# Attention with one query over 4096 keys: values matmuls on four column groups, a K pool of two buffers and a V pool of one

## The chip, the cores and the metric

One core of one Trainium2 chip. The metric is the device time in microseconds (us) of one execution, as the median of a kernel's runs. Single executions of one kernel mostly lie within 0.3% of each other. A profiled run's span is 1.7 us shorter than its reported time.

## The reference

```
B, H, Sq, Skv, Dh = 8, 32, 1, 4096, 128            # q, k, v in bfloat16
scores = einsum('bhqd,bhkd->bhqk', q, k) * Dh ** -0.5
out    = einsum('bhqk,bhkd->bhqd', softmax(scores), v)
```

There are 256 heads with one query each. K and V are 268.4 MB each and every byte is used once, so the kernel is a stream of 536.9 MB with some arithmetic beside it.

## The kernel before

Eight heads make a tile. A tile of K or V is 128 partitions x 256 rows x 128 numbers, 8.39 MB or 64 KiB per partition; there are 32 tiles of each (numbered 0 to 31). The kernel has three such buffers (192 KiB per partition) in SBUF, and its pool hands them out in turn to K and V. DVE multiplies K by the query and halves the sum over d, PE finishes that sum with identity matmuls, DVE and ACT make the softmax weights, and PE multiplies the weights by V ("values"): 64 matmuls per tile with 32 output columns each, then "pick" matmuls gather the right quarter of the 32 x 512 result.

```
SLOTS = 3
LAST = (8, 4)
...
    kv_pool = ctx.enter_context(tc.tile_pool(name="kv_pool", bufs=SLOTS))
...
    cuts = { ...                                    # pieces of a load, in rows of 256
        ("k", NT - 1): [C // 4, C // 4, C // 2],
        ("v", NT - 2): [C // 4] * 4,
        ("v", NT - 1): [C // 4] + [C // 8] * 4 + [24, 16, 12, *LAST],
    }
    def load(kind, t):
        src = k_t if kind == "k" else v_t
        buf = kv_pool.tile([P, C, D], BF16, name=f"{kind}t", tag="kv")
        ...                                         # one DMA per piece, all from SyncE
...
    def values_of(t, lo, hi):
        ...
        for c0 in range(lo, hi, CB):                # CB = 4 rows, 8 heads: 32 columns
            nc.tensor.matmul(
                avs[t][:], lhsT=w[:, c0 : c0 + CB, :], rhs=vt[:, c0 : c0 + CB, :],
                start=(c0 == 0), stop=...,
            )
...
        for t in range(NT):                         # Q = C // 4
            load("k", t + 1); load("v", t)
            product(t, 0, Q);      values_of(t - 2, 3 * Q, ...);  sum_over_d(t, 0)
            values_of(t - 2, ..., C); copy_of(t - 2)
            product(t, Q, 2 * Q);  sum_over_d(t, 1);  scores_of(t, 0)
            result_of(t - 2);      values_of(t - 1, 0, Q)
            product(t, 2 * Q, 3 * Q); sum_over_d(t, 2);  scores_of(t, 1)
            values_of(t - 1, Q, 2 * Q)
            product(t, 3 * Q, C);  sum_over_d(t, 3);  scores_of(t, 2); scores_of(t, 3)
            weights_of(t);         values_of(t - 1, 2 * Q, 3 * Q)
```

The loop is shortened here: the guards for the first and last tiles are left out. The order in it is the order on each engine. Values of one tile are spread over the time of two.

## Time and profile before

| | before |
|---|---|
| time, median of 6 runs | 1254.86 us (1254.75 to 1255.53) |
| span of the profiled run | 1253.2 us |
| first load packet / last V byte landed | 1.8 / 1249.2 us |
| one 64 KB packet on one DMA engine | 2.42 us (median of 7296) |

The first fence holds lines of the page of the kernel before: busy time by engine with its share of the span; the bandwidth in 40 equal slices of the span; the load queue with its share of the 16 DMA engines' time; two groups of instructions (busy us, mean ns of one, then the idle time before them and what ended it); the chain.

```profile
span 1253.2 us, 8139 instructions
PE 844.0 (67%) x3307; PEld 326.9 (26%) x3307; DVE 967.2 (77%) x531; ACT 341.1 (27%) x641; POOL 3.1 (0%) x17
...
GB/s 404 435 434 434 435 434 435 431 434 434 435 432 436 434 434 433 427 431 433 434 429 435 434 435 431 436 434 431 434 423 435 434 425 436 436 426 427 424 429 326
...
q1 hardware_dynamic: 12224, 536.94, 99.3%
...
DMA 59%; PE 32%; DVE 8%; ACT 1%; issue 0%; another core or an unknown queue 0%; SPq 0%
...
L173 DVE TENSOR_TENSOR kt<-kt,qb 128x8192 bf16<-128x8192 bf16 x128 | 565.1, 4415 | 137.2 <-DMA kt<-in_k_dram 130.3
L249 PE MATMUL av<-vt,w 128*32 128x512 bf16 x2045 | 529.8, 419 | 99.5 <-DMA vt<-in_v_dram 97.8
...
vt<-in_v_dram SPq DMA_DIRECT2D x30, 26.1
kt<-in_k_dram SPq DMA_DIRECT2D x27, 26.1
```

The load queue holds the 16 DMA engines for 99.3% of the span, and the bandwidth line is flat from the second slice to the last but one. DVE and PE both wait for loads, and yet the queue never runs empty. The chain gives PE 32%, but that is a matter of how it is followed back: a load waits for a buffer, the buffer for PE, PE for the load before it. What decides is whether the queue ever runs empty, and here it does not. The last two lines say that a whole load lands 26.1 us after its issue; as a tile takes 19.4 us to move, it was issued some 7 us before the queue would have emptied. I call that time the **lead** of a load.

The second fence is busy time by stretch at the end of the kernel before (window in us from the span's start, then the length, busy time and number of instructions per engine, granted PE clock, DMA share, GB/s).

```profile
core 0: us, PE busy (x) PEld busy (x) DVE busy (x) ACT busy (x) POOL busy (x), PEclk, DMA share, GB/s
1190.00:1228.00 38.00, 34.06 (x145) 13.85 (x144) 30.33 (x17) 10.43 (x18) 0.00 (x0) 0.90 1.01 428
1228.00:1233.00 5.00, 5.00 (x24) 2.15 (x23) 1.79 (x5) 2.59 (x9) 0.00 (x0) 1.00 0.98 413
1233.00:1249.00 16.00, 14.37 (x74) 6.39 (x72) 0.16 (x1) 7.25 (x25) 0.26 (x1) 1.00 0.84 345
1249.00:1254.00 5.00, 1.30 (x17) 0.90 (x15) 0.00 (x0) 0.94 (x2) 0.00 (x0) 0.85 0.00 1
```

DMA is full up to the last stretch, and PE works at full clock beside the last V tile. The fence is the timeline of PE in the middle of the kernel before (start, length, then the idle time before it).

```profile
606.59 5.30 PE L249 MATMUL av<-vt,w 128*32 128x512 bf16 x16 [3.51 <-DMA vt<-in_v_dram]
611.82 1.90 PE L188 MATMUL ps<-kt,ident 128*128 128x512 bf16 x8
613.65 3.63 PE L249 MATMUL av<-vt,w 128*32 128x512 bf16 x16
617.21 1.90 PE L188 MATMUL ps<-kt,ident 128*128 128x512 bf16 x8
619.04 5.35 PE L249 MATMUL av<-vt,w 128*32 128x512 bf16 x24
```

Sixteen values matmuls take 3.63 us once PE's clock is up and 5.30 us after idle time: 0.22 to 0.33 us each.

### The profile page before, as it was taken

Reading aid. Unit: us, or ns where it says so; the run is one execution under the profiler, and the core shown is the slowest. Engines: PE = TensorE matmul, PEld = TensorE weight load, DVE = VectorE, ACT = ScalarE, POOL = GpSimd, SP = SyncE. Lnnn points to the kernel's source line nnn. Section 1 sums busy time; section 2 is a strip of 40 time slices with the busy share of each in tenths; the row PEclk is TensorE's granted clock in tenths of the full one; section 3 lists DMA queues with packets and bytes.
Section 4 is the critical chain, followed back from the end, with each engine's and each line's share of the span. In section 5 each row is a group of like instructions: output and inputs, shape, how many; then the busy total and the mean of one; then the engine's idle time right before and its main releaser. Section 6 shows DMA issues by size and latency. Waiting matters only on the chain.

```text
span 1253.2 us, 8139 instructions
## 1 busy us (share of the span) xinstructions
PE 844.0 (67%) x3307; PEld 326.9 (26%) x3307; DVE 967.2 (77%) x531; ACT 341.1 (27%) x641; POOL 3.1 (0%) x17
## 2 busy tenths in 40 slices
PE   2466765768667685666765667765677667775788
PEld 0122222223222232222322222222222222222333
DVE  7877887777977779777788777886778877878991
ACT  0323033331233321333213322033220333313333
POOL 0000000000000000000000000000000000000000
PEclk8689787788778887788977888788887887887889
DMA  9999999999999999999999999999999999999997
GB/s 404 435 434 434 435 434 435 431 434 434 435 432 436 434 434 433 427 431 433 434 429 435 434 435 431 436 434 431 434 423 435 434 425 436 436 426 427 424 429 326
DMA packets 12598, 537.53 MB, mean 429 GB/s; under 512 B 1936, under 2 KB 2064, under 8 KB 2576
## 3 DMA queue, kind: packets, MB, share of 16 engines
q1 hardware_dynamic: 12224, 536.94, 99.3%
q8 instruction: 26, 0.43, 0.1%
q10 hardware_dynamic: 336, 0.07, 0.0%
q14 instruction: 12, 0.10, 0.0%
HBM read 536.94 MB, written 0.07 MB: 428 GB/s over the span
## 4 chain that ended last, share of the span: by engine, by line
DMA 59%; PE 32%; DVE 8%; ACT 1%; issue 0%; another core or an unknown queue 0%; SPq 0%
DMA vt<-in_v_dram 58%; PE av L249 22%; PE ps L188 10%; DVE kt L173 5%; DVE kt L176 2%; DMA q_all<-in_q_dram 1%; DVE sc L200 1%; ACT w L233 0%; DVE pmax L210 0%; DVE spread L212 0%; DVE nmax L217 0%; PE op L295 0%; ACT comb L284 0%; DVE bias L221 0%
## 5 line engine op out<-in xcount | busy, mean ns | idle before, releaser
L173 DVE TENSOR_TENSOR kt<-kt,qb 128x8192 bf16<-128x8192 bf16 x128 | 565.1, 4415 | 137.2 <-DMA kt<-in_k_dram 130.3
L249 PE MATMUL av<-vt,w 128*32 128x512 bf16 x2045 | 529.8, 419 | 99.5 <-DMA vt<-in_v_dram 97.8
L188 PE MATMUL ps<-kt,ident 128*128 128x512 bf16 x1024 | 303.6, 450 | 273.6 <-DVE kt L176 273.3
L233 ACT ACTIVATE w<-sc,bias 128x256 bf16<-128x256 f32 (+1 forms) x264 | 301.1, 1557 | 532.3 <-DVE bias L221 532.3
L249 PEld LDWEIGHTS <-w 128*32 128x32 bf16 x2045 | 206.6, 105 | 418.5 <-issue 238.9
L176 DVE TENSOR_TENSOR kt<-kt 128x4096 bf16<-128x4096 bf16 x128 | 293.3, 2292 | 4.4
L188 PEld LDWEIGHTS <-ident 128*128 128x128 bf16 x1024 | 105.5, 109 | 469.1 <-issue 347.8
L200 DVE TENSOR_REDUCE sc<-ps 128x64 f32<-128x512 f32 x128 | 87.6, 685 | 114.9 <-PE ps L188 114.9
L233 ACT ACTIVATION_READ_ACCUMULATOR w<-sc,bias 128x1 f32 x264 | 130.8, 495 | 0.0
L284 ACT ACTIVATE comb<-av 32x512 bf16<-32x512 f32 x32 | 19.1, 597 | 236.6 <-PE qh L157 158.6
L306 ACT ACTIVATE stage<-op,rz 16x128 bf16<-16x128 f32 x16 | 5.7, 358 | 112.1 <-DVE rz L271 111.3
L163 PE MATMUL qp<-qg,heads 8*128 8x128 bf16 x32 | 6.9, 214 | 24.8 <-ACT qg L161 24.8
L210 DVE TENSOR_REDUCE pmax<-sc 128x1 f32<-128x256 f32 x32 | 13.4, 420 | 1.1
L161 ACT ACTIVATE qg<-qh 8x128 bf16<-8x128 f32 x32 | 8.1, 252 | 18.3 <-PE qh L157 18.3
L157 PE MATMUL qh<-q_all,ident 128*8 128x128 bf16 x32 | 7.2, 224 | 8.4 <-DMA q_all<-in_q_dram 8.4
L295 PE MATMUL op<-comb,pick 32*16 32x128 bf16 x128 | 12.3, 215 | 0.2 <-ACT comb L284 0.2
L271 DVE RECIPROCAL rz<-zp 16x1 f32<-16x1 f32 x16 | 2.3, 147 | 12.1 <-PE zp L263 12.1
L165 ACT ACTIVATE qb<-qp 128x128 bf16<-128x128 f32 x32 | 8.9, 278 | 9.6 <-PE qp L163 9.6
L212 DVE TENSOR_SCALAR spread<-same,pmax 128x32 f32<-128x32 f32 x32 | 7.7, 242 | 1.1
L295 PEld LDWEIGHTS <-pick 32*16 32x16 bf16 x128 | 6.6, 83 | 7.0 <-issue 6.6
L221 DVE TENSOR_SCALAR bias<-own,nmax 128x8 f32<-128x8 f32 x32 | 7.4, 230 | 1.1
L217 DVE TRANSPOSE_TENSOR_REDUCE nmax<-spread 128x1 f32<-128x32 f32 x32 | 6.8, 212 | 1.1
(29 smaller groups left out, 18.1 us busy)
## 6 DMA issues: line engine op xcount, KB each, us to landing
kt<-in_k_dram SPq DMA_DIRECT2D x8, 4096.0 KB, 25.5
vt<-in_v_dram SPq DMA_DIRECT2D x5, 2048.0 KB, 27.1
kt<-in_k_dram SPq DMA_DIRECT2D x4, 2048.0 KB, 15.2
vt<-in_v_dram SPq DMA_DIRECT2D x4, 1024.0 KB, 25.8
vt<-in_v_dram SPq DMA_DIRECT2D x1, 768.0 KB
vt<-in_v_dram SPq DMA_DIRECT2D x1, 512.0 KB, 21.8
vt<-in_v_dram SPq DMA_DIRECT2D x30, 26.1
kt<-in_k_dram SPq DMA_DIRECT2D x27, 26.1
```

Of the source, the lines that this page charges most:

```text
L161: nc.scalar.activation(out=qg[:], in_=qh[:], func=ACT.Copy)
L165: nc.scalar.activation(out=qb[:, 0, :], in_=qp[:], func=ACT.Copy)
L173: nc.vector.tensor_tensor(out=part, in0=part, in1=qb[:].to_broadcast([P, MC, D]), op=ALU.mult)
L176: nc.vector.tensor_tensor(out=part[:, :, 0 : D // 2], in0=part[:, :, 0 : D // 2], in1=part[:, :, D // 2 : D], op=ALU.add,)
L188: nc.tensor.matmul(ps[:], lhsT=ident[:], rhs=kt[:, u * UC : (u + 1) * UC, s * DS : (s + 1) * DS], start=(s == 0), stop=(s == n - 1),)
L200: nc.vector.tensor_reduce(out=scs[t][:, u * UC : (u + 1) * UC], in_=sums.pop((t, u))[:], axis=AX.X, op=ALU.add)
L210: nc.vector.tensor_reduce(out=pmax[:], in_=sc[:], axis=AX.X, op=ALU.max)
L212: nc.vector.tensor_scalar(out=spread[:], in0=same[:], scalar1=pmax[:, 0:1], scalar2=-scale, op0=ALU.add, op1=ALU.mult,)
L233: nc.scalar.activation(out=w[:, c0 : c0 + n, g], in_=sc[:, c0 : c0 + n], func=ACT.Exp, bias=bias[:, g : g + 1], scale=scale, accum_out=esu ...
L249: nc.tensor.matmul(avs[t][:], lhsT=w[:, c0 : c0 + CB, :], rhs=vt[:, c0 : c0 + CB, :], start=(c0 == 0), stop=(c0 + CB == (C if t < NT - 1 e ...
L284: nc.scalar.activation(out=comb[:], in_=avs.pop(t)[:], func=ACT.Copy)
L295: nc.tensor.matmul(ops[n][:], lhsT=pick[:, m, r, :], rhs=comb[:, m * D : (m + 1) * D], start=(r == 0 and m == 0), stop=(r == R - 1 and m = ...
```

## The change

The intent: fill the array. A values matmul has 32 output columns, so four of them fit side by side on four column groups, each into its own quarter of the PSUM tile's partitions. With the values of a tile done in one short burst, V needs its buffer for hardly longer than the load itself, so one V buffer is enough and K can have two.

```
-SLOTS = 3
+KB, VB = 2, 1
+TG = 4
-LAST = (8, 4)
+LAST = 4
...
-    kv_pool = ctx.enter_context(tc.tile_pool(name="kv_pool", bufs=SLOTS))
+    k_pool = ctx.enter_context(tc.tile_pool(name="k_pool", bufs=KB))
+    v_pool = ctx.enter_context(tc.tile_pool(name="v_pool", bufs=VB))
...
-        ("v", NT - 2): [C // 4] * 4,
-        ("v", NT - 1): [C // 4] + [C // 8] * 4 + [24, 16, 12, *LAST],
+        ("v", NT - 1): [C // 2, C // 4, C // 8, C // 16, C // 32, LAST, LAST],
...
         for c0 in range(lo, hi, CB):
+            j = c0 // CB % TG
             nc.tensor.matmul(
-                avs[t][:], lhsT=w[:, c0 : c0 + CB, :], rhs=vt[:, c0 : c0 + CB, :],
-                start=(c0 == 0), stop=(c0 + CB == (C if t < NT - 1 else C - NL)),
+                avs[t][j * AG : (j + 1) * AG, :], lhsT=w[:, c0 : c0 + CB, :],
+                rhs=vt[:, c0 : c0 + CB, :], start=(c0 < CB * TG), stop=(c0 + CB * TG >= end),
             )
...
     def copy_of(t):                                # last tile: half by ACT, half by DVE
-        nc.scalar.activation(out=comb[:], in_=avs.pop(t)[:], func=ACT.Copy)
+        n = CB if t < NT - 1 else CB // 2
+        nc.scalar.activation(out=comb[:, 0:n, :], in_=av[:, 0:n, :], func=ACT.Copy)
+        if n < CB:
+            nc.vector.tensor_copy(out=comb[:, n:CB, :], in_=av[:, n:CB, :])
...
+            v_last = t >= NT - 2
...
             sum_over_d(t, 1)
             scores_of(t, 0)
+            if t > 0 and not v_last:
+                values_of(t - 1, 0, C)             # the whole burst, behind the 2nd score sum
+                copy_of(t - 1)
...
             sum_over_d(t, 3)
             scores_of(t, 2)
+            if t > 0 and v_last:
+                values_of(t - 1, 0, C)             # last two tiles: behind the 4th
             scores_of(t, 3)
```

All values of tiles t-2 and t-1 that stood between these lines go. The copied tile is 128 x 512 instead of 32 x 512, at the same number of pick matmuls. A second accumulator for the last softmax sums, and some pieces of the last rows, go too.

More of the change, by code (lines that the diff above doesn't have):

```diff
@@ L48 @@
     TB = 32
-    NL = sum(LAST)
-    assert NH % P == 0 and P % G == 0 and TB % PH == 0 and C % CB == 0
+    AG = CB * G
+    assert TG * AG == P and NH % P == 0 and P % G == 0 and TB % PH == 0 and C % CB == 0
     q_n = q.rearrange("b h o d -> (b h o) d").rearrange("(x p) d -> p x d", p=P)
@@ L104 @@
     )
-    pick = consts.tile([CB * G, CB, R, RG], BF16, name="pick")
+    pick = consts.tile([P, CB, R, RG], BF16, name="pick")
     nc.gpsimd.memset(pick[:], 0.0)
-    nc.gpsimd.affine_select(
-        out=pick[:], in_=pick[:], pattern=[[-G, CB], [G, R], [-1, RG]],
-        compare_op=ALU.not_equal, fill=1.0, base=0, channel_multiplier=1,
-    )
-    nc.gpsimd.affine_select(
-        out=pick[:], in_=pick[:], pattern=[[-G, CB], [0, R], [0, RG]],
-        compare_op=ALU.is_ge, fill=0.0, base=0, channel_multiplier=1,
-    )
-    nc.gpsimd.affine_select(
-        out=pick[:], in_=pick[:], pattern=[[G, CB], [0, R], [0, RG]],
-        compare_op=ALU.is_ge, fill=0.0, base=G - 1, channel_multiplier=-1,
-    )
+    for j in range(TG):
+        part = pick[j * AG : (j + 1) * AG, :, :, :]
+        nc.gpsimd.affine_select(
+            out=part, in_=part, pattern=[[-G, CB], [G, R], [-1, RG]],
+            compare_op=ALU.not_equal, fill=1.0, base=0, channel_multiplier=1,
+        )
+        nc.gpsimd.affine_select(
+            out=part, in_=part, pattern=[[-G, CB], [0, R], [0, RG]],
+            compare_op=ALU.is_ge, fill=0.0, base=0, channel_multiplier=1,
+        )
+        nc.gpsimd.affine_select(
+            out=part, in_=part, pattern=[[G, CB], [0, R], [0, RG]],
+            compare_op=ALU.is_ge, fill=0.0, base=G - 1, channel_multiplier=-1,
+        )
     ones = consts.tile([P, 1], F32, name="ones")
     nc.vector.memset(ones[:], 1.0)
-    late = consts.tile([P, R, G], F32, name="late")
-    nc.vector.memset(late[:], 0.0)
-    w_last = consts.tile([P, NL, RG], BF16, name="w_last")
+    w_last = consts.tile([P, LAST, RG], BF16, name="w_last")
     nc.gpsimd.memset(w_last[:], 0.0)
@@ L141, in load @@
         src = k_t if kind == "k" else v_t
-        buf = kv_pool.tile([P, C, D], BF16, name=f"{kind}t", tag="kv")
+        pool = k_pool if kind == "k" else v_pool
+        buf = pool.tile([P, C, D], BF16, name=f"{kind}t", tag=kind)
         c0 = 0
@@ L227, in weights_of @@
         esum = esums[t // R]
-        n = C // 2 if t == NT - 1 else C
-        for c0 in range(0, C, n):
-            if c0 > 0:
-                esum = late
-            for g in range(G):
-                nc.scalar.activation(
-                    out=w[:, c0 : c0 + n, g], in_=sc[:, c0 : c0 + n], func=ACT.Exp,
-                    bias=bias[:, g : g + 1], scale=scale, accum_out=esum[:, t % R, g : g + 1],
-                )
+        for g in range(G):
+            nc.scalar.activation(
+                out=w[:, :, g], in_=sc[:], func=ACT.Exp, bias=bias[:, g : g + 1], scale=scale,
+                accum_out=esum[:, t % R, g : g + 1],
+            )
         ws[t] = w
         if t == NT - 1:
-            nc.gpsimd.tensor_copy(out=w_last[:, :, RG - G : RG], in_=w[:, C - NL : C, :])
+            nc.gpsimd.tensor_copy(out=w_last[:, :, RG - G : RG], in_=w[:, C - LAST : C, :])
     avs = {}
@@ L246, in values_of @@
         if lo == 0:
-            avs[t] = ps_v.tile([CB * G, CB * D], F32, name="av", tag="av")
+            avs[t] = ps_v.tile([P, CB * D], F32, name="av", tag="av")
+        end = C if t < NT - 1 else C - LAST
         for c0 in range(lo, hi, CB):
+            j = c0 // CB % TG
             nc.tensor.matmul(
-                avs[t][:], lhsT=w[:, c0 : c0 + CB, :], rhs=vt[:, c0 : c0 + CB, :],
-                start=(c0 == 0), stop=(c0 + CB == (C if t < NT - 1 else C - NL)),
+                avs[t][j * AG : (j + 1) * AG, :], lhsT=w[:, c0 : c0 + CB, :],
+                rhs=vt[:, c0 : c0 + CB, :], start=(c0 < CB * TG), stop=(c0 + CB * TG >= end),
             )
@@ L260, in norm_of @@
         zp = ps_z.tile([RG, 1], F32, name="zp", tag="zp")
-        parts = [esums.pop(n)] + ([late] if n == NQ - 1 else [])
-        for i, e in enumerate(parts):
-            nc.tensor.matmul(
-                zp[:], lhsT=e.rearrange("p r g -> p (r g)"), rhs=ones[:],
-                start=(i == 0), stop=(i == len(parts) - 1),
-            )
+        nc.tensor.matmul(
+            zp[:], lhsT=esums.pop(n).rearrange("p r g -> p (r g)"), rhs=ones[:],
+            start=True, stop=True,
+        )
         zps[n] = zp
@@ L273 @@
     combs = {}
-    def last_rows(n, lo, hi):
-        for i in range(lo, hi):
-            nc.tensor.matmul(
-                ops[n][:], lhsT=w_last[:, i, :], rhs=loads["v", NT - 1][:, C - NL + i, :],
-                start=False, stop=(i == NL - 1),
-            )
-    def copy_of(t):
-        comb = small.tile([CB * G, CB * D], BF16, name="comb", tag="comb")
-        nc.scalar.activation(out=comb[:], in_=avs.pop(t)[:], func=ACT.Copy)
+    def copy_of(t):
+        comb = small.tile([P, CB, D], BF16, name="comb", tag="comb")
+        av = avs.pop(t)[:].rearrange("p (m d) -> p m d", d=D)
+        n = CB if t < NT - 1 else CB // 2
+        nc.scalar.activation(out=comb[:, 0:n, :], in_=av[:, 0:n, :], func=ACT.Copy)
+        if n < CB:
+            nc.vector.tensor_copy(out=comb[:, n:CB, :], in_=av[:, n:CB, :])
         combs[t] = comb
@@ L292, in result_of @@
         if t == NT - 1:
-            last_rows(n, 0, LAST[0])
+            for i in range(LAST):
+                nc.tensor.matmul(
+                    ops[n][:], lhsT=w_last[:, i, :], rhs=loads["v", t][:, C - LAST + i, :],
+                    start=False, stop=False,
+                )
         for m in range(CB):
             nc.tensor.matmul(
-                ops[n][:], lhsT=pick[:, m, r, :], rhs=comb[:, m * D : (m + 1) * D],
-                start=(r == 0 and m == 0), stop=(r == R - 1 and m == CB - 1 and t < NT - 1),
-            )
-        if t == NT - 1:
-            last_rows(n, LAST[0], NL)
+                ops[n][:], lhsT=pick[:, m, r, :], rhs=comb[:, m, :],
+                start=(r == 0 and m == 0), stop=(r == R - 1 and m == CB - 1),
+            )
     def finish_of(n):
@@ L311, in finish_of @@
             lo = u if (last and u == OB - 1) else 0
-            n = RG // 2 if last and lo == 0 else RG
-            for x in range(0, RG, n):
-                nc.scalar.dma_start(
-                    o_n[s, x : x + n, lo : u + 1, :], stages[s][x : x + n, lo : u + 1, :]
-                )
+            nc.scalar.dma_start(o_n[s, :, lo : u + 1, :], stages[s][:, lo : u + 1, :])
     Q = C // 4
@@ L322 @@
         for t in range(NT):
-            late_v = t >= NT - 3
+            v_last = t >= NT - 2
+            n = t // R - 1
             if t + 1 < NT:
@@ L327 @@
             product(t, 0, Q)
-            if t > 1:
-                values_of(t - 2, 3 * Q, 3 * Q + Q // 2)
             sum_over_d(t, 0)
-            if t > 1:
-                values_of(t - 2, 3 * Q + Q // 2, C)
-                copy_of(t - 2)
+            if t > 2 and t % R == 1:
+                recip_of(n)
+                finish_of(n)
             if t + 1 < NT:
@@ L338 @@
             scores_of(t, 0)
-            if t > 1:
-                if t % R == 1:
-                    norm_of(t // R - 1)
-                result_of(t - 2)
-            if t > 0 and (t == NT - 1 or not late_v):
-                values_of(t - 1, 0, Q)
+            if t > 0 and not v_last:
+                values_of(t - 1, 0, C)
+                copy_of(t - 1)
             product(t, 2 * Q, 3 * Q)
@@ L347 @@
             scores_of(t, 1)
-            if t > 1 and t % R == 1:
-                recip_of(t // R - 1)
-                finish_of(t // R - 1)
-            if t > 0 and (t == NT - 1 or not late_v):
-                values_of(t - 1, Q, 2 * Q)
             product(t, 3 * Q, C)
-            done = 0 if late_v else 2 * Q
-            if t == NT - 1:
-                done = 2 * Q + Q // 2
-                values_of(t - 1, 2 * Q, done)
             sum_over_d(t, 3)
             scores_of(t, 2)
+            if t > 0 and v_last:
+                values_of(t - 1, 0, C)
             scores_of(t, 3)
@@ L362 @@
             if t > 0:
-                values_of(t - 1, done, 3 * Q)
-        values_of(NT - 2, 3 * Q, C)
-        copy_of(NT - 2)
+                if v_last:
+                    copy_of(t - 1)
+                if t % R == 0:
+                    norm_of(n)
+                result_of(t - 1)
         values_of(NT - 1, 0, C // 2)
@@ L368 @@
         recip_of(NQ - 1)
-        result_of(NT - 2)
-        values_of(NT - 1, C // 2, C - NL)
+        values_of(NT - 1, C // 2, C - LAST)
         copy_of(NT - 1)
```

## The prediction

> **What bounds it now.** DMA. The page's queue table gives the load queue 99.3% of the 16 DMA engines' span. Packet records show loads streaming without a gap from 1.8 us to 1249.3 us: 536.9 MB at 430 GB/s, 433.5 GB/s in undisturbed stretches (one 64 KB packet per engine each 2.42 us). The Trainium skill ("DMA: Bandwidth & Descriptors", Specifications) puts the fabric ceiling at 435 GB/s; the trace agrees. An 8.39 MB tile takes 19.4 us, a K+V pair 38.7 us. DVE (77% busy) and PE (67%) don't bind. What is not streaming is 1.8 us of head and 3.9 us of tail (last V byte 1249.2, end 1253.2), so no change to compute can win over 0.5%; it can only lose by leaving the queue empty. The time is 1.8 us above the span.
>
> **What the change does.**
> 1. Values matmuls go to four column groups. Today 64 in a row cost 222 ns each warm, 14.2 us (timeline: 29 in 6.43 us), 420 cold. The skill ("TensorE: Matmul & The Clock Gate", Part 3) says different column groups run concurrently, 2.38x for three; no run here shows it. Pick matmuls show that a weight-load/matmul pair can issue every 58 ns. Estimate: 64 in 4 to 7 us, mean start to start 60 to 110 ns.
> 2. V has one buffer: the load of V(t) now waits for all values matmuls of t-1 (the program's semaphore value is that of the 64th). K has two.
> 3. Values of t-1 run in one burst after the second score sum of t.
> 4. Copies are 128x512 instead of 32x512, same ACT time (0.59 us); the last is split over ACT and DVE. Small steps removed: under 1 us.
>
> **Middle.** V(t-1) lands at L, K(t+1) at L+19.4. DVE's products for half of K(t) end about L-6, their sums L-3. The burst runs L to L+6, V(t) is issued about L+6, 13 us before the queue would empty. K(t+2) is issued about L+12, 26 us before. Even unpacked (14 to 17 us) the queue would just stay fed. No gain, no loss: still 38.7 us per pair.
>
> **End.** After K(31) there is no K left to cover the wait. V(30) is one load landing at about 1229 (now its last piece lands at 1229.3). Then: burst of 64 matmuls (5.5 us; the scores of tile 31 may add 1), wake, issue and first packet 1.3 us (first load: issue 0.8, first packet 1.8), V(31) in 19.5 us instead of following on. Last byte about 1255 instead of 1249.2; tail 3.9 us, maybe 0.2 less. Fewer small loads win back about 0.5 us (rate falls to 422 to 428 GB/s after 1210 today). Net +6 us: span 1259.3, time 1261 us. Range 1257.5 to 1267. Chances: faster 0.01, within 2% 0.96, slower 0.03.
>
> **What the profile should show.** GB/s slices unchanged up to the last two; a hole of 6 to 8 us without load packets at about 1229 to 1236, and no other; the SyncE wait of the first V(31) piece ended by a values matmul; issue-to-landing about 32 us for V, about 45 for K (now 26 for both); values matmuls overlapping, PE busy far below 844 us; DVE idle still ended by the K load; tail after the last byte under 4 us.
>
> **What would make it wrong.** No overlap between column groups: hole 15 us, time about 1270. Bursts on a half clock (above 17 us): holes in every pair, over 100 us lost. V(31) released piece by piece: no hole, time 1254. A DMA rate that depends on queue depth.

## The result, and the profile after

| | before | after |
|---|---|---|
| time, median of 6 runs | 1254.86 us | 1259.93 us (1259.68 to 1261.88) |
| ratio, 95% interval | | 1.0042 [1.0029, 1.0055] |
| span of the profiled run | 1253.2 | 1258.3 |
| V(29) landed | 1188.99 | 1189.13 |
| V(30) landed | 1229.34 | 1227.98 |
| last V byte landed | 1249.21 | 1253.83 |
| from there to the end of the span | 4.0 | 4.4 |

Ratios in this document are the mean time of one kernel's runs over that of the other's of the same rounds, so not quite the ratio of the medians quoted. The interval says that it is 0.3 to 0.6% slower.

The landing rows already hold most of the answer. Sixty of the 64 tiles come before V(29), and at its landing the two kernels are 0.14 us apart. Everything happens in the three tiles after it. The lines of the page after that answer to those of before:

```profile
span 1258.3 us, 8134 instructions
PE 551.6 (44%) x3299; PEld 201.1 (16%) x3299; DVE 967.6 (77%) x531; ACT 343.2 (27%) x625; POOL 6.0 (0%) x26
...
GB/s 402 433 434 434 434 433 433 434 434 434 433 435 432 434 432 432 433 432 432 432 432 433 434 432 434 432 432 433 434 432 433 433 433 432 430 432 430 430 410 268
...
q1 hardware_dynamic: 11360, 536.94, 98.9%
...
DMA 79%; PE 15%; DVE 6%; issue 0%; SPq 0%; another core or an unknown queue 0%; ACT 0%
...
L174 DVE TENSOR_TENSOR kt<-kt,qb 128x8192 bf16<-128x8192 bf16 x128 | 565.2, 4415 | 187.0 <-DMA kt<-in_k_dram 180.4
L248 PE MATMUL av<-vt,w 128*32 128x512 bf16 x2047 | 176.0, 517 | 92.3 <-DMA vt<-in_v_dram 92.2
...
vt<-in_v_dram SPq DMA_DIRECT2D x31, 33.3
kt<-in_k_dram SPq DMA_DIRECT2D x27, 47.4
```

The packing works: 2047 values matmuls keep PE busy 176.0 us instead of 529.8, though the mean of one has risen to 517 ns. Busy time far below count times mean is how overlap looks on this page. PE's total falls by 292 us, and the time does not fall at all: PE was not what the kernel waited for. Only in its last two slices does the bandwidth line fall more than 4 GB/s below that of before: 410 and 268 against 429 and 326. The leads have grown: 33.3 - 19.4 = 14 us for V, 28 us for K.

The same stretches at the end, after:

```profile
1190.00:1228.00 38.00, 20.21 (x110) 7.39 (x109) 31.02 (x19) 10.23 (x18) 0.00 (x0) 0.73 0.93 401
1228.00:1233.00 5.00, 3.64 (x64) 1.72 (x65) 1.52 (x5) 3.31 (x7) 0.00 (x0) 1.00 0.34 95
1233.00:1254.00 21.00, 7.71 (x71) 2.90 (x71) 0.16 (x1) 6.53 (x13) 0.21 (x1) 0.61 0.90 378
1254.00:1259.00 5.00, 1.20 (x9) 0.57 (x6) 0.42 (x1) 0.74 (x2) 0.00 (x0) 0.50 0.00 1
```

In the second stretch DMA moves 95 GB/s instead of 413. In it stand exactly the 64 values matmuls of tile 30. The chain of the kernel after, in order of time (start, length, what), shows how they come to stand there:

```profile
1197.05 30.93 DMA vt<-in_v_dram
1227.98 0.04 issue
1228.03 3.67 PE av L248 x64
1231.69 0.02 issue
1231.71 0.33 SPq L146
...
1233.56 19.61 DMA vt<-in_v_dram
```

And SyncE's waits after 1200 us (what waited for whom, us in total, times, longest):

```profile
SPq L146 <- DMA vt<-in_v_dram: 30.6, 1, 30.6
...
SPq L146 <- PE av L248: 3.7, 1, 3.7
```

V(31) needs the one V buffer. It is free when V(30) has landed (1227.98) and been multiplied (1231.67); everywhere else a K load fills that time, but after K(31) there is no K left. The last load packet of V(30) ends at 1227.54 and the first of V(31) starts at 1232.67: a hole of 5.1 us.

The sum, from the table and these lines, of the 5.0 us between the spans: V(30) lands 1.36 us earlier; +4.69 from there to the first packet of V(31) (burst 3.7, issue to first packet 1.0); V(31) takes 21.16 us from that packet to its last byte, where it took 19.87 behind V(30) before: +1.29; the work after the last byte is 0.42 us longer. -1.36 + 4.69 + 1.29 + 0.42 = 5.04.

### The profile page after: what moved, and what is told of

It reads as the page before. It is cut to its first block, busy times and chain, and to the rows that moved or that the text cites. A ratio compares the mean times of both kernels' runs of the same rounds, so it can differ in the third digit from the quotient of the medians.

```text
span 1258.3 us, 8134 instructions
## 1 busy us (share of the span) xinstructions
PE 551.6 (44%) x3299; PEld 201.1 (16%) x3299; DVE 967.6 (77%) x531; ACT 343.2 (27%) x625; POOL 6.0 (0%) x26
## 4 chain that ended last, share of the span: by engine, by line
DMA 79%; PE 15%; DVE 6%; issue 0%; SPq 0%; another core or an unknown queue 0%; ACT 0%
DMA vt<-in_v_dram 78%; PE av L248 14%; DVE kt L174 3%; DVE kt L177 2%; PE ps L189 1%; DMA q_all<-in_q_dram 1%; DVE sc L201 0%; SPq L146 0%; DVE pmax L211 0%; DVE spread L213 0%; DVE nmax L218 0%; DVE comb L278 0%; ACT comb L276 0%; PE op L293 0%
## 5 line engine op out<-in xcount | busy, mean ns | idle before, releaser
L174 DVE TENSOR_TENSOR kt<-kt,qb 128x8192 bf16<-128x8192 bf16 x128 | 565.2, 4415 | 187.0 <-DMA kt<-in_k_dram 180.4
L189 PE MATMUL ps<-kt,ident 128*128 128x512 bf16 x1024 | 351.8, 506 | 574.0 <-DVE kt L177 574.0
L230 ACT ACTIVATE w<-sc,bias 128x256 bf16<-128x256 f32 x256 | 300.5, 1587 | 252.2 <-DVE bias L222 252.2
L189 PEld LDWEIGHTS <-ident 128*128 128x128 bf16 x1024 | 119.5, 119 | 776.3 <-issue 500.6
L248 PE MATMUL av<-vt,w 128*32 128x512 bf16 x2047 | 176.0, 517 | 92.3 <-DMA vt<-in_v_dram 92.2
L276 ACT ACTIVATE comb<-av 128x512 bf16<-128x512 f32 (+1 forms) x32 | 19.5, 609 | 422.0 <-PE av L248 422.0
L230 ACT ACTIVATION_READ_ACCUMULATOR w<-sc,bias 128x1 f32 x256 | 126.7, 495 | 0.0
L248 PEld LDWEIGHTS <-w 128*32 128x32 bf16 x2047 | 67.2, 125 | 211.0 <-DMA vt<-in_v_dram 109.4
L293 PE MATMUL op<-comb,pick 128*16 128x128 bf16 x128 | 13.1, 226 | 16.6 <-ACT comb L276 16.5
L293 PEld LDWEIGHTS <-pick 128*16 128x16 bf16 x128 | 7.4, 90 | 23.8 <-issue 23.7
## 6 DMA issues: line engine op xcount, KB each, us to landing
vt<-in_v_dram SPq DMA_DIRECT2D x1, 2048.0 KB, 16.6
vt<-in_v_dram SPq DMA_DIRECT2D x1, 512.0 KB, 19.4
vt<-in_v_dram SPq DMA_DIRECT2D x31, 33.3
```

Of the source, the lines that this page charges most:

```text
L174: nc.vector.tensor_tensor(out=part, in0=part, in1=qb[:].to_broadcast([P, MC, D]), op=ALU.mult)
L189: nc.tensor.matmul(ps[:], lhsT=ident[:], rhs=kt[:, u * UC : (u + 1) * UC, s * DS : (s + 1) * DS], start=(s == 0), stop=(s == n - 1),)
L230: nc.scalar.activation(out=w[:, :, g], in_=sc[:], func=ACT.Exp, bias=bias[:, g : g + 1], scale=scale, accum_out=esum[:, t % R, g : g + 1],)
L248: nc.tensor.matmul(avs[t][j * AG : (j + 1) * AG, :], lhsT=w[:, c0 : c0 + CB, :], rhs=vt[:, c0 : c0 + CB, :], start=(c0 < CB * TG), stop=(c ...
L276: nc.scalar.activation(out=comb[:, 0:n, :], in_=av[:, 0:n, :], func=ACT.Copy)
L293: nc.tensor.matmul(ops[n][:], lhsT=pick[:, m, r, :], rhs=comb[:, m, :], start=(r == 0 and m == 0), stop=(r == R - 1 and m == CB - 1),)
```

## The experiments

The theory: the hole before V(31), made by the single V buffer, is the whole loss, and the middle is level because V's lead is long enough. The rivals: the loss comes from the fewer, larger last pieces and the longer work after the last byte; or packing or the two pools slow the stream; or packing itself changes something. Eight kernels were built and run; all gave correct results. They were run in two rounds, and the kernel before ran beside each: median 1254.85 us (9 runs) beside V(31) in the K buffer, V(30) in four pieces, one column group and the column groups alone; 1255.14 us (9 runs) beside the other four.

### Last V tile in the K buffer that is free by then

```
-        pool = k_pool if kind == "k" else v_pool
-        buf = pool.tile([P, C, D], BF16, name=f"{kind}t", tag=kind)
+        home = "k" if kind == "k" or t == NT - 1 else "v"
+        pool = k_pool if home == "k" else v_pool
+        buf = pool.tile([P, C, D], BF16, name=f"{kind}t", tag=home)
```

> The changed kernel, but the last V tile takes the K buffer that is free by then. Theory (the whole loss is the hole before the last V tile, made by the single V buffer): no stretch without load packets near the end, the last byte lands about 1247.5 to 1248.5 us (1228.0, where the second-last V tile landed, plus 19.5), 5 to 6 us before the changed kernel's 1253.8; span about 1252 us, time 1253.5 to 1254.5, so level with the kernel before or up to 0.1% faster. Rival 1 (the loss is in the fewer, larger last pieces and the longer work after the last byte): time stays at 1259 to 1260. Rival 2 (packing or the two pools slow the stream in the middle): the second-last tiles land later than in the kernel before, and time stays over 1257.

Measured: 1254.96 us (1254.52 to 1255.19), ratio to the kernel before 1.0000 [0.9987, 1.0012]. Its stretches at the end:

```profile
1190.00:1228.00 38.00, 19.61 (x117) 7.28 (x119) 31.27 (x19) 10.24 (x18) 0.00 (x0) 0.74 1.00 433
1228.00:1233.00 5.00, 3.34 (x64) 1.53 (x57) 0.75 (x4) 4.11 (x7) 0.00 (x0) 1.00 1.03 439
```

The burst of 64 stands where it stood, and DMA now moves 439 GB/s beside it. The last byte lands at 1248.68 us. Freeing V(31) from V(30)'s buffer gives back 5.0 of the 5.1 us, with the larger pieces, the packing and both pools kept. That settles the cause of the loss. My two numbers were still a little too good: the last byte is 0.2 us later than the expected range and the time 0.5 us above it. The V(31) load lands 21.0 us after V(30) here too, without any hole, so 21 us are not a cost of the restart alone. In this trace the 16 DMA engines are out of step: the first packet of V(31) starts at 1222.20 us, 5.5 us before V(30) lands. A load lands with its slowest engine, so from landing to landing is not what the load takes on an engine.

### Second-last V load in four pieces again

```
+        ("v", NT - 2): [C // 4] * 4,
         ("v", NT - 1): [C // 2, C // 4, C // 8, C // 16, C // 32, LAST, LAST],
```

> The changed kernel with the second-last V load cut into four pieces as in the kernel before. Theory: smaller packets (16 KB take 0.613 us against 2.42 us for 64 KB, 1.3% slower) make the tile land 0.2 to 0.4 us later; the burst stands behind the last score sums either way, so the hole is the same and the time is 1260 to 1260.5. Rival (one whole load is what makes the hole, since nothing can start before all of it is there): the burst would start earlier in pieces and the time falls by 2 us or more.

Measured: 1259.23 us (1258.49 to 1259.76), ratio to before 1.0033 [1.0021, 1.0046]. Neither line holds. V(30) lands at 1228.04, not later than the whole load, and the burst starts at 1227.38 instead of 1228.03, right behind the last score sums, because most of its pieces have landed. So the single load costs 0.65 us here and no more: the score sums of tile 31 end only then. The last byte lands 0.69 us earlier than after. The piece size is a small part of the loss, and a part of the hole, not a cause beside it.

### Values on one column group

```
-TG = 4
+TG = 1
...                      # pick, av and comb get TG * AG = 32 partitions
```

> The changed kernel with all values matmuls in one column group. Theory: the hole is the burst of 64 values matmuls plus about 1 us of issue plus a slow restart; unpacked the burst is 14 to 17 us instead of 3.6, so the hole grows from 5 to about 16 us and the time to 1270 to 1273. The middle stays fed, just: V is issued 2 to 5 us before the queue empties. Rival (the single V buffer would not have worked without packing): holes in every pair of tiles, V issued after the queue is empty, time over 1300.

Measured: 1302.8 us (1299.13 to 1311.54; the profiled run has a span of 1297.3), ratio 1.0404 [1.0375, 1.0434]. My own number is missed by 30 us, and the rival is not right either: its time came, but not its reason. The trace shows no moment with an empty queue before 1219 us, yet V(29) lands 11.1 us later than after. The wait of SyncE on the values grows:

```profile
SPq L146 <- DMA vt<-in_v_dram: 629.4, 31, 22.1
SPq L146 <- PE av L248: 451.1, 30, 16.8
```

In the kernel after, the second line was 166.4 us. One burst takes 14.0 to 16.6 us; one of them in the timeline:

```profile
689.13 13.99 PE L248 MATMUL av<-vt,w 128*32 128x512 bf16 x64 [1.74 <-DMA vt<-in_v_dram]
```

So V is issued with a lead of 2.6 to 6.7 us instead of 12.8 to 17.1. At the end there are two real holes, 8.2 us before V(30) and 18.1 us before V(31), where the kernel after has one of 5.1, because for the last two tiles the burst stands behind the fourth score sum. The unpacked values also make the work after the last byte longer, 9.9 us instead of 4.4. The 11 us of the middle needed an explanation, which the next experiment tests.

### The burst behind the fourth score sum for every tile

```
-            v_last = t >= NT - 2
+            v_last = t > 0
```

> The changed kernel, packed, with the values burst of every tile behind the fourth score sum instead of the second, as the change does for the last two tiles only. Theory (what the unpacked run lost in the middle is not packing itself but the lead: a load issued under about 5 us before the queue's end costs 0.2 to 1.2 us, with no visible hole): V is issued about 16 us after the last V landed, so with a lead of 3 to 4 us, 64 KB packets longer than 2.5 us become many (over 200, against 51), and the second-last tile lands 6 to 20 us later than 1189 (tile 29); time 1266 to 1280. Rival (any lead above 1 us, the time from issue to first packet, is enough, and the unpacked run lost its 11 us to something else): time 1259 to 1261.

Measured: 1278.55 us (1276.26 to 1280.15), ratio 1.0185 [1.0169, 1.0201], slower; V(29) lands at 1206.30, 17.2 us later than after; between 60 and 1180 us, 442 packets of 64 KB take over 2.5 us, against 51. The theory's numbers hold, with packing on. From the bandwidth line of this run:

```profile
GB/s 404 452 415 422 415 425 443 411 428 428 425 430 425 425 425 429 430 423 417 436 432 420 430 422 433 428 413 440 405 430 425 424 427 411 448 425 423 425 406 264
```

The line is restless from the second slice on, though its DMA share is 9 tenths or more in every slice but the last: the loss does not look like a hole. From the packet records between 60 and 1180 us, per DMA engine: what 64 KB packets took beyond 2.42 us each adds up to 12.9 us against 1.8 after, and idle time to 7.3 us against 0.6. Together 17.8 us more, for the 17.2 us of V(29). For the unpacked run the same sums give 8.4 + 3.2 = 11.6 us for its 11.1. (The packet records do not name their engine; packets were joined end to start into 16 rows to find the idle time.)

Sorted by lead (here from the issue of a V load to the landing of the K load before it), the packets of over 2.5 us that start within 6 us of that landing:

| lead of the V load | runs | loss by stretched packets, per load |
|---|---|---|
| 2.2 to 4.0 us | late burst 16, one group 11 | 0.05 to 1.18 us, 26 of 27 at 0.23 or more |
| 4.1 to 4.7 us | late burst 8, one group 3 | 0.01 to 0.92 us |
| 5.1 to 7.0 us | late burst 3, one group 15, before 23 | 0.00 to 0.42 us, 37 of 41 under 0.1 |
| 8 us and more | before, after, late burst | 0.00 to 0.06 us |

The kernel before ran with leads of 5.5 to 8.6 us (once 11.6), just outside the costly range. That a short lead costs is shown by two runs that came to it in different ways. Why the limit lies near 5 us is shown only in part.

The 16 engines report the end of a load one by one, and the trace holds these times, so one can see how far they are out of step. In the kernel after, the first engine ends its part of a V load 1.5 us before the last early in the run, and 5.0 us at V(30). With short leads the engines stay closer: 0.4 to 3.3 us in the late-burst run. From the issue of a load to its first packet takes 1.0 us more. So the first engines can run dry though the lead of the load as a whole is not used up. Reckoned from these times (an engine reports 0.4 us after its last packet), that happened at 22 of the 58 V loads of the late-burst and one-group runs in this window, and at each of the 22 the packet records show idle engines. In the kernels before and after it happened at none. The one load with a lead over 5 us that lost 0.42 us is among the 22: the engines were 4.1 us apart there.

That is not the whole account. The idle times reckoned so are about half of the added idle time, and the stretched packets are the larger part of the loss. They start mostly 0 to 5 us after the issue. Packets that reach an idle engine are long (behind the hole of the kernel after, the first 32 KB packets took 1.37 to 2.12 us, against 1.215 usually), but loads at which no engine ran dry lost up to 0.9 us in long packets too. Why these were long stays open, and the limit is not a sharp one: some leads near 4 us cost almost nothing.

### The two pools alone, in the kernel before

```
-SLOTS = 3
+KB, VB = 2, 1
...                      # k_pool and v_pool in load(), as in the change
```

> The kernel before with two buffers for K and one for V, nothing else changed: values still unpacked and spread over two tiles' time. Theory (the V buffer must be free before the K load in flight ends; the new order of the values burst is what makes one V buffer possible): the last quarter of the values of a tile runs after the next tile's first product, about 11 us after K has landed, with the queue empty from then on; a hole of 11 to 14 us in every pair, time 1600 to 1720. Rival (the shared pool was only a matter of form): time under 1290.

Measured: 1698.9 us (one timed and one profiled run), ratio 1.354. Its bandwidth line shows the holes that a short lead alone does not make:

```profile
GB/s 421 371 321 269 275 321 371 272 272 272 395 317 277 247 346 369 273 272 272 396 298 271 272 346 371 271 273 272 396 297 272 272 347 369 255 339 321 396 401 292
```

The packet records hold a hole of 13.5 to 14.8 us in 26 of the 32 pairs of tiles. So the parts of the change are not independent: one V buffer needs the values in one early burst, as the change does it. Packing then sets V's lead, 13 to 14 us against 2.6 to 6.7 unpacked.

### The four column groups alone, in the kernel before

```
-        avs[t][:], lhsT=w[:, c0 : c0 + CB, :], rhs=vt[:, c0 : c0 + CB, :],
-        start=(c0 == 0), ...
+        avs[t][j * AG : (j + 1) * AG, :], lhsT=w[:, c0 : c0 + CB, :], rhs=vt[:, c0 : c0 + CB, :],
+        start=(c0 < CB * TG), ...       # av, comb and pick as in the change; pools, order, cuts as before
```

> The kernel before with the values matmuls spread over four column groups, nothing else changed. Theory (PE is off the critical path in the middle): PE busy falls from 844 us to below 650, the time stays within 0.1% of the kernel before, 1254 to 1256. Rival (packing itself costs or gains, through the clock or through reads that slow the loads): a difference over 0.2%.

Measured: 1255.09 us (1255.01 to 1255.25), ratio 1.0001 [0.9989, 1.0014]; PE busy 596.0 us instead of 844.0. A quarter of a millisecond of PE work is gone and the time is the same. Packing neither gains nor costs by itself, within the interval.

### The work after the last byte: one whole copy, and a warm PE

Both build on the first experiment (V(31) in a K buffer).

```
-        n = CB if t < NT - 1 else CB // 2
-        nc.scalar.activation(out=comb[:, 0:n, :], in_=av[:, 0:n, :], func=ACT.Copy)
-        if n < CB: nc.vector.tensor_copy(out=comb[:, n:CB, :], in_=av[:, n:CB, :])
+        nc.scalar.activation(out=comb[:], in_=av[:], func=ACT.Copy)
```

> The changed kernel with the last V tile in the free K buffer and the last copy out of PSUM done whole by ACT instead of half by ACT and half by DVE. In the traces the DVE half starts only when the ACT half has ended (0.38 + 0.42 us, against 0.59 us whole). Theory: the work after the last byte gets 0.1 to 0.3 us shorter; time 1254.5 to 1255.0. Rival: the copy is hidden behind the last-row matmuls, no change.

The second adds 4, 6 and 3 unread matmuls of 128 x 512 between the last V pieces.

> As whole_copy, with 13 matmuls that nobody reads between the last V pieces, so that PE stays busy. Theory (a part of the longer work after the last byte is PE at a granted clock of 0.5 to 0.6, values matmuls of 0.61 us against 0.38): the granted clock of the last 10 us rises to 0.9 or more, time from last V byte to end falls from 4.1 to 3.6 us; time 1254.0 to 1254.7, below the kernel before by up to 0.05%. Rival: the clock doesn't matter to the few matmuls left; no change.

Measured: 1254.72 us (1254.52 to 1255.09), ratio 0.9997 [0.9985, 1.0010], and 1254.60 us (1254.38 to 1254.84), ratio 0.9996 [0.9984, 1.0009]. Neither differs from the kernel before, or from the first experiment, beyond the interval. The profile says more. In the kernel after the two half copies run one behind the other (start, length, and what ended the wait):

```profile
1254.18 0.38 ACT L276 ACTIVATE comb<-av 128x256 bf16<-128x256 f32 x1 [14.65 <-PE av L248]
1254.60 0.42 DVE L278 CAST comb<-av 128x256 bf16<-128x256 f32 x1 [6.91 <-ACT comb L276]
```

Whole, the copy is one piece of 0.60 us. Both times lie in their expected ranges, but the expectation that the whole copy makes the work after the last byte shorter was missed: 4.3 us, against 4.1 in the first experiment. The last 5 us of the warm kernel:

```profile
1249.00:1254.00 5.00, 0.85 (x15) 0.46 (x7) 0.00 (x0) 0.95 (x2) 0.00 (x0) 1.00 0.00 1
```

The granted clock is 1.00 there, against 0.50 after, and from the end of the last values matmul to the start of the last scaling takes 1.1 us against 1.3 in the kernel after. But the last byte is followed by the output's DMA after 2.1 us, as after (2.0): the three last unread matmuls, started at 1247.88, still ran when the next-to-last pieces landed, and took back what the clock gave. The expectation of 3.6 us from the last byte to the end was missed; it was 4.5. What the clock is worth can be read from the other traces instead. In the kernel before and in the first experiment, whose end is that of the kernel after line for line, the granted clock was 1.00 at the last byte, and the last scaling starts 1.35 and 1.33 us after that byte. In the kernel after, the four-piece, late-burst, whole-copy and column-groups-alone runs it was 0.50, and the scaling starts 1.62 to 1.68 us after it. So some 0.3 us of the 0.4 us of longer end go with the clock; the rest lies after the landing of the output. In the first experiment the clock was up by chance: its profiled run is the fastest of the five.

## Why the prediction was right, and where it was not

- **The bound, and no gain from PE.** Right. The prediction said that compute could not win over 0.5%. PE lost 292 us of busy time and the time rose by 0.4%; packing alone changed it by 0.01% +- 0.13%. Where the expected gain of packing went: PE was off the critical path, and its freed time became idle time in front of the loads (DVE's idle time before K loads rose from 130.3 to 180.4 us as well).
- **The mechanism of the loss.** Right. "After K(31) there is no K left to cover the wait": one hole, at the predicted place, ended by the values of tile 30, and moving V(31) into a K buffer removes it with its whole cost.
- **The size.** 1261 predicted, 1259.93 measured, by terms that partly cancel, so a part of this closeness is luck. The hole was put at 6 to 8 us and was 5.1. V(30) was said to land at "about 1229", and landed at 1228.0. The burst was put at 5.5 us with up to 1 more; it took 3.7, because the score sums of tile 31 end just before it, so PE's clock is up (in the middle of the kernel, after idle time, a burst takes 5.0 to 6.5 us). "Wake, issue and first packet 1.3 us" was 1.0. V(31) "in 19.5 us" was 21.2: the estimate overlooked that the first packets behind an empty queue are 0.2 to 0.9 us longer, and that the pieces of V(31) get smaller; how the 1.7 us divide is left open. The tail was said to be 3.9 us or less and is 4.4.
- **The middle.** The result, level, was right: V(29) lands within 0.14 us, leads of 13 to 14 us as predicted, issue to landing 33 us for V and 47 for K (said: about 32 and 45). One sentence was wrong: "Even unpacked (14 to 17 us) the queue would just stay fed. No gain, no loss". Unpacked, V still had 3 to 6 us of lead and the time was 1302.8 us, not the 1270 given for "no overlap between column groups". A lead was treated as safe whenever it was longer than the way from issue to first packet. The runs show a loss at leads up to 4.7 us, and hardly any from 5.1 us on; engines that end a load before its landing are a part of the reason, the rest is open.
- **Column groups overlap.** Right: in the warm burst the matmul starts come in fours, 2 to 5 ns apart, the fours 0.22 us apart; 64 take 3.64 us against 14.0 us on one column group (the line shown for that run), so 3.8 times as fast. This agrees with the Trainium skill, "TensorE: Matmul & The Clock Gate", Part 3, which gives about 4 ns per tile of the array and measured three column groups.
- **"Fewer small loads win back about 0.5 us".** Partly: V(30) landed 1.4 us earlier than before, but neither of the two differences makes that alone: in four pieces with no V(31) queued behind it V(30) landed at 1228.04, whole with V(31) queued at 1227.66, and only with both, as before, at 1229.34. Why is left open.

## What to carry to other kernels

In a kernel that streams, ask of each buffer what other load is in flight while it waits to be free, and ask it separately for the last tile: a single buffer that is covered by the other stream in the steady state is bare at the end, and a free buffer of the other pool closes that hole at no cost. Judge a load by its lead (how long before the queue would run empty it is issued): here leads of 5.5 us and more cost 0.13 us at most in stretched packets, and leads of 2 to 4 us cost up to 1.2 us each, without a visible hole. A faster engine that the kernel was not waiting for buys room for buffers and order, not time.

## What the Trainium skill lacked or had wrong

- "DMA: Bandwidth & Descriptors" (Rules for kernel authors) says to issue a DMA early and wait late, but gives no lead. Here V loads of 8.39 MB lost 0.05 to 1.18 us each at leads of 2.2 to 4.0 us in stretched packets (64 KB in over 2.5 us instead of 2.42), and at most 0.13 us at 5.5 us and more, while the DMA share showed no hole. No page gives a time by which the 16 engines of one load can be out of step: here the first ended its part of an 8.39 MB load 0.4 to 5.0 us before the last, with a spread that grew from 1.5 to 5.0 us in the course of the kernel after.
- The same page (Specifications) gives a ceiling of 435 GB/s; 64 KB packets give 16 x 65536 B / 2.42 us = 433.3 GB/s, which agrees. It has no measured rates by packet size for such loads; in the kernel before, 32 KB took 1.215 us, 16 KB 0.612, 8 KB 0.312 and 1 KB 0.046, that is 431.5, 428, 420 and 356 GB/s.
- "TensorE: Matmul & The Clock Gate" (Part 3) gives 2.38x for three column groups of 512 columns and no measured figure for four; here four gave 3.8x (64 matmuls in 3.64 us against 14.0 us on one).
- "TensorEngine Tiling (Array Packing)" (PSUM Bottleneck) advises to use both ScalarE and VectorE for PSUM evacuation. On one PSUM tile it did not help here: DVE's half waited for ACT's (0.38 + 0.42 us, against 0.60 whole). "PSUM — Partial Sum Buffer" (Terms) names a possible reason, two engines on the same bank and quadrant at once are an error; no run here tests whether that is why DVE waited.
